# One core, long convolution plus token MLP: shift copies and norm subtractions go to GpSimd, one token group's output pairs go last, and the written order is new

## The chip, the cores and the metric

The kernel runs on one core of a Trainium2 chip. The metric is the device time of one execution in microseconds (us). The engines are TensorE (PE, with its weight loads shown as PEld), VectorE (DVE), ScalarE (ACT), GpSimd (POOL) and SyncE (SP, which issues most DMA transfers). Line numbers are those of the kernel before, as its profile shows them.

## The reference

Two mixers work on the same input x = A_q, of 2048 tokens and 640 features, and a gate blends them:

```python
x = A_q
g = _sigmoid((x * gate_w).sum(-1, keepdims=True))
a = _A_ref(x, A_k, A_v, A_shift_k, A_ssm_k, A_ssm_D)
b = _B_ref(x, B_w1, B_w2, B_w3, B_w4)
return g * a + (1 - g) * b
```

Mixer A filters k along the tokens with four taps, multiplies by v (kv), convolves kv over all tokens with a filter of 2048 taps per feature (in the reference by FFT), adds kv times ssm_D and multiplies by q. Mixer B takes h = gelu(layernorm(x) @ w1), shifts the four quarters of h's features by +1, -1, +2 and -2 tokens, multiplies by w2 and adds x; of this x1 it takes gelu(layernorm(x1) @ w3) @ w4 and adds x1. Weights and inputs are bf16.

## The kernel before

Tokens lie in 16 tiles of 128 partitions, and in four groups sc of four tiles. The steps:

- ln1 normalizes x (statistics on DVE, `bn_math` at line 864 on POOL, with a power -0.5 by `pool_pow` at line 861) and transposes it, by PE for tiles 0 to 7 and by a transposing DMA afterwards.
- mm1 (line 910) is h = gelu(xn @ w1) for five feature tiles of 128. Each of the first four holds 128 features of one quarter; the fifth holds the remaining 32 features of every quarter. The shift of the first four costs nothing, since mm2 reads them at an offset. The fifth has four shifts in one tile, so after its gelu on ACT four copies of 32 partitions go to it at four offsets (line 924, on DVE): 24 copies in all, 16 of 256 columns and 8 of 512.
- mm2(t) (line 945) is x1 = x + h @ w2; it reads the fifth feature tile with its copies. ln2(t) normalizes x1: `ln_math` (line 868) makes -mean, mean squared less epsilon, the difference (line 872, a DVE instruction of one column), and its power -0.5, in 128x1 instructions on POOL but for that one; tiles 0 to 7 are then scaled on DVE, the rest on ACT.
- mm3 and mm4 (lines 976 and 997) are the MLP of 1536 features. `base` (line 992) scales x1 by 1 - g and stores it to the output; mm4's result is scaled on ACT and added to the output by an accumulating POOL transfer (line 1005). Where a half of a tile is not stored by `base` ("summed" is false), mm4 adds x1 by a matmul with the identity.
- The convolution is a transform over blocks of 512 tokens: h_load, h_fold and h_chunk for the filter, kv_block, x_fwd and combine for kv, in two halves hh of 320 features. unit(hh, c) multiplies block c with the filter's blocks on DVE (128x2560 products); two of its sums are accumulating POOL transfers inside SBUF (line 1029).
- final(hh, c, q, k) (line 1053) is the inverse transform of a pair of token tiles, 4c+q and 4c+3-q: two blocks of four matmuls, an ACT copy, two DVE additions, a flip by one matmul with a reversed identity, an ACT copy with the gate's scale, a DVE product with q. For k < 12 the pair is added to the output by an accumulating POOL transfer (line 1078). The last four, k = 12 to 15, are added on DVE to the scaled mm4 result that lies in SBUF, and stored by SP (lines 1080 and 1081); for k = 14 and 15 these last steps are done tile by tile. k goes through hh = 0, then 1, and in each through c = 3, 2, 1, 0.

All operations are recorded first. The order in which each engine runs them is a list, SEQUENCE, written out by hand: `schedule` (line 271) walks it with a model of durations, which gives PSUM banks and some extra waits, and `emit` writes the instructions in that order, each with the semaphore waits that its data need. Every engine works in order, so an instruction that waits holds all behind it. Nearly all instructions have a helper's line: tt 669, ts 674, act 679, mm 689, dma 237 (plain) and 234 (transposing).

Of the kernel before, what the change touches and what calls it, by code (L numbers as in the profile page):

```python
# [8 lines left out]
ACTF = mybir.ActivationFunctionType  # L9
# [3 lines left out]
class Op:  # L13
    __slots__ = ("idx", "eng", "fns", "ins", "outs", "dur", "bias", "nbytes", "preds", "succs", "rank",
                 "tp", "early", "cost", "free", "grp", "tile", "ordinal", "waits", "inc", "value", "dsem", "dval", "snap", "snapd", "start", "end", "order", "lat")

    def __init__(self, idx, eng, fns, ins, outs, dur, bias, nbytes):
        self.idx = idx
        self.eng = eng
        self.fns = fns  # L20
        self.ins = ins
        self.outs = outs
        self.dur = dur
        self.bias = bias
        self.nbytes = nbytes
        self.preds = {}
        self.succs = []
        self.inc = False
        self.dsem = None
        self.tp = False  # L30
        self.early = False
        self.cost = 0.0
        self.lat = 0.0
        self.free = None
        self.tile = None
# [87 lines left out]
def regions(ap):  # L123
# [29 lines left out]
    out = set()  # L153
    for lo, hi in runs:
        b0, b1 = (f0 + lo) * esz, (f0 + hi) * esz
        for q in range(p0 // 32, (p0 + pcnt - 1) // 32 + 1):
            out.add(("SB", q, b0, b1))
# [16 lines left out]
class Prog:  # L174
# [51 lines left out]
    def dma(self, queue, out, in_, bias=0.0, transpose=False, slow=False, free=None, early=False, accum=False, fn=None):  # L226
# [11 lines left out]
        issue = (350.0 + n / 90.0) if transpose else (970.0 if queue == "pool" else 470.0)  # L238
# [5 lines left out]
        op.cost = n * esz / 256 * 1.65 if transpose else n * esz / run * ((46 + 0.087 * run) if accum else (8 + 0.0435 * run)) / 16  # L244
# [26 lines left out]
    def schedule(self, sequence, backlog=3000.0):  # L271
# [4 lines left out]
        done = []  # L276
        avail = [0.0] * 8
# [4 lines left out]
        for i in sequence:  # L282
            o = ops[i]
            st = max([free[o.eng]] + [ops[p].end + d for p, d in delays[i]])
            if o.nbytes and not o.tp and not o.early:
                st = max(st, dfree - backlog)
            t = o.tile
# [15 lines left out]
            if o.nbytes:  # L303
                dfree = max(st + 0.5 * o.dur, dfree) + o.cost
                o.end = max(dfree, o.end) + o.lat
                if o.cost > 500 and not o.tp and not o.early:
# [157 lines left out]
def bass_gated_mix__ssm_conv_h3__mixer_s_mlp__prompt_kernel(  # L464
# [33 lines left out]
    def ps(n, cls):  # L498
# [3 lines left out]
    SEQUENCE = [2, 3, 10, 11, 12, 31, 6, 57, 8, 1, 13, 14, 15, 16, 17, 18, 19, 20, 21, 22, 23, 24, 25, 7, 9, 0, 4, 28, 5, 56, 29, 63, 58, 64,  # L502
# [482 lines left out]
    def summed(hh, t):  # L985
        return 8 * hh + 2 * (3 - t // 4) < KACC
# [200 lines left out]
```

## Time and profile before

| what | value |
|---|---|
| median of the runs shown | 235.55 us (234.9 to 235.9, 3 runs) |
| profiled execution, device time | 235.56 us |
| profiled execution, span | 233.8 us |
| granted TensorE clock, mean | 0.994 |
| ACT busy, instructions | 170.3 us, 317 |
| POOL busy, instructions | 105.9 us, 122 |
| DMA, mean | 195 GB/s |

The span is the time from the first to the last instruction. Busy time counts an engine's own work, not its waiting. A group of instructions has the form: line, engine, operation, out<-in with shapes, xcount, then busy us, mean ns of one, and idle time of the engine just before them with what ended it. In a timeline the columns are start, length, engine, line, operation, with idle time before in square brackets. A row of the waits reads: who waited, for whom, total us, times, longest.

### The profile page before, as it was taken

Reading aid. Unit: us, or ns where it says so; the run is one execution under the profiler, and the core shown is the slowest. Engines: PE = TensorE matmul, PEld = TensorE weight load, DVE = VectorE, ACT = ScalarE, POOL = GpSimd, SP = SyncE. Lnnn points to the kernel's source line nnn. Section 1 sums busy time; section 2 is a strip of 40 time slices with the busy share of each in tenths; the row PEclk is TensorE's granted clock in tenths of the full one; section 3 lists DMA queues with packets and bytes.
Section 4 is the critical chain, followed back from the end, with each engine's and each line's share of the span. In section 5 each row is a group of like instructions: output and inputs, shape, how many; then the busy total and the mean of one; then the engine's idle time right before and its main releaser. Section 6 shows DMA issues by size and latency. Waiting matters only on the chain.

```text
span 233.8 us, 4171 instructions
## 1 busy us (share of the span) xinstructions
PE 221.1 (95%) x1501; PEld 134.6 (58%) x1501; DVE 220.1 (94%) x402; ACT 170.3 (73%) x317; POOL 105.9 (45%) x122
## 2 busy tenths in 40 slices
PE   7999999989998999999999999999999999999960
PEld 2598665436554656544775456654666556776630
DVE  6998999999988999998999999999989999979994
ACT  2799699488796899769949897577655387288881
POOL 0330406274495801196376693246024332456870
PEclk9999999999999999999999999999999999999997
DMA  5999959898878999978638988999978987989998
GB/s 161 360 345 250 253 146 271 246 277 204 140 181 176 240 213 317 343 212 180 157 97 145 187 189 163 146 191 206 259 142 145 196 140 142 185 98 111 95 109 165
DMA packets 63785, 45.48 MB, mean 195 GB/s; under 512 B 28818, under 2 KB 59028, under 8 KB 63764
## 3 DMA queue, kind: packets, MB, share of 16 engines
q1 hardware_dynamic: 54748, 33.33, 55.2%
q0 software_dynamic: 8832, 11.80, 34.9%
q8 instruction: 12, 0.20, 0.3%
q10 hardware_dynamic: 184, 0.08, 0.1%
q14 instruction: 9, 0.07, 0.1%
HBM read 24.22 MB, written 6.55 MB: 132 GB/s over the span
## 4 chain that ended last, share of the span: by engine, by line
PE 45%; DVE 9%; POOL 3%; ACT 2%; issue 1%
PE PSall L689 45%; DVE arena L669 8%; ACT arena L679 2%; POOL arena L674 1%; POOL arena L861 1%; POOL arena L669 1%; DVE arena L959 0%; DVE arena L674 0%
## 5 line engine op out<-in xcount | busy, mean ns | idle before, releaser
L689 PE MATMUL PSall<-arena 128*128 128x320 bf16 (+5 forms) x1444 | 213.7, 307 | 5.3 <-DVE arena L669 2.4
L669 DVE TENSOR_TENSOR arena<-arena 128x640 bf16<-128x640 bf16 (+5 forms) x247 | 182.3, 793 | 3.0 <-ACT arena L679 1.9
L689 PEld LDWEIGHTS PSall<-arena 128*128 128x128 bf16 (+1 forms) x1444 | 130.5, 98 | 86.9 <-DVE arena L669 4.2
L679 ACT ACTIVATE arena<-PSall 128x512 bf16<-128x512 f32 (+6 forms) x189 | 107.7, 634 | 29.4 <-PE PSall L689 25.2
L679 ACT ACTIVATE arena<-arena 128x640 bf16<-128x640 bf16 (+4 forms) x62 | 42.2, 703 | 6.7 <-POOL arena L669 2.7
L861 POOL TENSOR_TENSOR arena<-arena 128x1 f32<-128x1 f32 (+1 forms) x26 | 29.3, 1128 | 31.9 <-DVE arena L674 31.5
L674 POOL TENSOR_SCALAR arena<-arena 128x1 f32<-128x1 f32 (+2 forms) x41 | 24.8, 608 | 34.7 <-DVE arena L959 12.0
L237 POOL DMA_DIRECT2D out_dram<-arena x28 | 30.5, 1197 | 20.5 <-ACT arena L679 15.0
L679 ACT ACTIVATE arena<-PSall,arena 128x640 bf16<-128x640 f32 (+1 forms) x32 | 20.6, 658 | 20.0 <-PE PSall L689 19.9
L237 POOL DMA_DIRECT2D arena<-arena x12 | 14.9, 1242 | 32.1 <-DVE arena L669 28.2
L674 DVE TENSOR_SCALAR arena<-arena 128x640 bf16<-128x640 bf16 (+2 forms) x49 | 14.4, 307 | 3.4 <-POOL arena L674 1.6
L857 DVE BATCH_NORM_STATS2 arena<-arena 128x6 f32<-128x320 bf16 x32 | 14.6, 479 | 2.0 <-DMA arena<-in_A_q_dram 1.7
L669 POOL TENSOR_TENSOR arena<-arena 128x1 f32<-128x1 f32 (+1 forms) x11 | 10.3, 943 | 2.9 <-DVE arena L674 2.5
L715 PE MATMUL PSall<-arena 128*128 128x512 bf16 x15 | 5.4, 536 | 1.6 <-DVE arena L711 1.6
L959 DVE SCALAR_TENSOR_TENSOR arena<-PSall,arena 128x640 bf16<-128x640 f32 x8 | 6.4, 808 | 0.1
L924 DVE TENSOR_SCALAR arena<-arena 32x256 bf16<-32x256 bf16 (+1 forms) x24 | 5.9, 244 | 0.5
L679 ACT ACTIVATE PSall<-PSall 128x640 f32<-128x640 f32 x8 | 5.6, 699 | 0.1
L715 PEld LDWEIGHTS PSall<-arena 128*128 128x128 bf16 x15 | 1.9, 132 | 4.6 <-issue 2.5
L903 PE MATMUL PSall<-arena 128*128 128x128 bf16 x40 | 3.6, 219 | 0.3
L718 ACT ACT_TABLE_LOAD x1 | 1.3, 1283 | 2.7 <-issue 2.7
L903 PEld LDWEIGHTS PSall<-arena 128*128 128x128 bf16 x40 | 2.4, 97 | 1.4 <-DVE arena L858 0.4
L858 DVE BATCH_NORM_AGGREGATE arena<-arena 128x2 f32<-128x12 f32 x16 | 3.0, 197 | 0.0
(24 smaller groups left out, 9.6 us busy)
## 6 DMA issues: line engine op xcount, KB each, us to landing
arena<-arena POOLq DMA_DIRECT2D x12, 640.0 KB, 6.3
arena<-in_A_k_dram SPq DMA_DIRECT2D x14, 400.0 KB, 4.1
arena<-in_A_q_dram SPq DMA_DIRECT2D x14, 320.0 KB, 6.9
out_dram<-arena POOLq DMA_DIRECT2D x20, 160.0 KB, 4.2
arena<-in_A_ssm_k_dram SPq DMA_DIRECT2D x5, 512.0 KB, 4.4
arena<-in_A_v_dram SPq DMA_DIRECT2D x16, 160.0 KB, 3.9
arena<-in_B_w_dram SPq DMA_DIRECT2D x1, 1920.0 KB, 8.8
out_dram<-arena SPq DMA_DIRECT2D x10, 160.0 KB, 3.7
```

What stands on the lines that cost most here:

```text
L237: fn = lambda e: e.dma_start(out, in_, **kw)
L669: P.op(eng, lambda e: e.tensor_tensor(o, real(a), real(b), op), [a, b], [o], dve_ns(o, [a, b], 2) if eng == "dve" else 500)
L674: P.op(eng, lambda e: e.tensor_scalar(o, real(a), s1, s2, op0=op0, **({} if op1 is None else {"op1": op1})), [a] + aps, [o], dve_ns(o, [a] ...
L679: P.op("act", lambda e: e.activation(real(o), real(a), f, bias=bias, scale=scale, **({"accum_out": accum} if accum is not None else {})), ...
L689: fns.append(lambda e, l=l, r=r, i=i: e.matmul(real(o), l, r, start=(i == 0), stop=(i == last)))
L715: P.op("pe", lambda e: e.matmul(real(pw), warm[:, 0:128], warm[:, 128:640], start=True, stop=True), [warm], [pw], 427.0 if i < 14 else 216.0)
L857: P.op("dve", lambda e, o=o, i=i: e.bn_stats(o, i), [i], [o], 400)
L858: P.op("dve", lambda e: e.bn_aggr(bna[:, t, :], bns[k]), [bns[k]], [bna[:, t, :]], 120)
L861: P.op("pool", lambda g: g.tensor_tensor(o, a, e, ALU.pow), [a, e], [o], dur)
L903: P.op("pe", [lambda e, c=c, pb=pb, xn=xn: e.transpose(real(pb)[:, 128 * c:128 * (c + 1)], xn[:, 128 * c:128 * (c + 1)], ident) for c in r ...
L924: P.op("dve", lambda e, o=hT[q, 4, c0:c0 + n], i=hx[q, :]: e.tensor_scalar(o, i, 1.0, None, op0=ALU.mult), [hx[q, :]], [hT[q, 4, c0:c0 + n ...
L959: P.op("dve", lambda e: e.scalar_tensor_tensor(x, real(pr), 1.0, x, op0=ALU.mult, op1=ALU.add, accum_out=st[1, 0][:, t:t + 1]), [pr, x], [ ...
```

## The change

1. `mm1`: for groups 1 to 3 the four shift copies are POOL transfers from SBUF to SBUF (16 in all); group 0 keeps its 8 DVE copies.
2. `ln_math`: the subtraction of one column goes from DVE to POOL.
3. `summed(hh, t)` is true for tiles 0 to 11 and false for 12 to 15, in both halves, where it was true everywhere but for the second half of tiles 0 to 7. So `base` and mm4's accumulating transfer leave tiles 12 to 15 out and take all 640 columns elsewhere; x1 of tiles 12 to 15 is added by the identity matmul.
4. `final` runs with k over c = 2, 1, 0 in both halves, then c = 3 in both halves, so that the four pairs summed on DVE are those of tiles 12 to 15.
5. SEQUENCE is a new list. The durations that `schedule` assumes are changed, and it limits the outstanding transfers in its model; regions of SBUF are rounded to 4 bytes when dependencies are found; a gelu waits for the first one.

```diff
 def regions(ap):
...
-        b0, b1 = (f0 + lo) * esz, (f0 + hi) * esz
+        b0, b1 = (f0 + lo) * esz // 4 * 4, ((f0 + hi) * esz + 3) // 4 * 4
...
+        tab = [tjunk[:, 1:2]] if f == ACTF.Gelu_apprx_tanh else []
...
-        ts(s[3], s[1], s[4], None, ALU.subtract)
+        tt(s[3], s[1], s[4], ALU.subtract, eng="pool")
         pool_pow(s[5], s[3], neghalf[:, t:t + 1])
...
                 for g in range(4):
                     c0, q = 2 + SHIFT[g] + t0, slice(32 * g, 32 * (g + 1))
+                    if sc >= 1:
+                        P.dma("pool", hT[q, 4, c0:c0 + n], hx[q, :])
+                        continue
...
     def summed(hh, t):
-        return 8 * hh + 2 * (3 - t // 4) < KACC
+        return t < 12
 
     def tile_rows(t):
-        n = 640 if summed(1, t) else 320
-        return X[:, t, 0:n], out[0, 128 * t:128 * (t + 1), 0:n]
+        return X[:, t, :], out[0, 128 * t:128 * (t + 1), :]
 
     def base(t):
+        if t >= 12:
+            return
...
-        x, o = tile_rows(t)
-        P.dma("pool", o, x, accum=True)
+        if t < 12:
+            x, o = tile_rows(t)
+            P.dma("pool", o, x, accum=True)
...
-        full, gy, ab = qb[k % 8], gyb[k % 8], (abb[k % 4] if k < 12 else abl[k - 12])
+        full, gy, ab = qb[2 * ((2 - c) % 4) + q], gyb[k % 8], (abb[k % 4] if k < 12 else abl[k - 12])
...
-    for hh in range(2):
-        for c in (3, 2, 1, 0):
-            for q in range(2):
-                at(final, hh, c, q, 8 * hh + 2 * (3 - c) + q)
+    k = 0
+    for group in ((2, 1, 0), (3,)):
+        for hh in range(2):
+            for c in group:
+                for q in range(2):
+                    at(final, hh, c, q, k)
+                    k += 1
...
-    SEQUENCE = [2, 3, 10, 11, 12, 31, 6, 57, 8, 1, 13, 14, 15, 16, 17, 18, 19, 20, 21, 22, 23, 24, 25, 7, 9, 0, 4, 28, 5, 56, 29, 63, 58, 64,
...
+    SEQUENCE = [10, 11, 12, 13, 14, 15, 16, 17, 4, 18, 19, 1, 7, 0, 2, 5, 3, 9, 8, 6, 56, 61, 20, 21, 31, 57, 30, 59, 60, 27, 64, 62, 63, 28,
...
```

In the new order PE runs the fifteen warm-up matmuls partly among the first real ones; the inverse matmuls of the first half's groups 2, 1 and 0 stand before the last quarter of mm3; and mm4 of tiles 12 to 15 stands at the end, the last 13 matmuls of tile 12 being PE's last.

More of the change, by code (lines that the diff above doesn't have):

```diff
@@ L14 @@
     __slots__ = ("idx", "eng", "fns", "ins", "outs", "dur", "bias", "nbytes", "preds", "succs", "rank",
-                 "tp", "early", "cost", "free", "grp", "tile", "ordinal", "waits", "inc", "value", "dsem", "dval", "snap", "snapd", "start", "end", "order", "lat")
+                 "tp", "early", "cost", "free", "grp", "tile", "ordinal", "waits", "inc", "value", "dsem", "dval", "snap", "snapd", "start", "end", "order", "lat", "ring")
     def __init__(self, idx, eng, fns, ins, outs, dur, bias, nbytes):
@@ L33, in __init__ @@
         self.lat = 0.0
+        self.ring = 0
         self.free = None
@@ L237, in dma @@
             fn = lambda e: e.dma_start(out, in_, **kw)
-        issue = (350.0 + n / 90.0) if transpose else (970.0 if queue == "pool" else 470.0)
+        issue = (1240.0 + n / 1200.0) if transpose else 970.0 if queue == "pool" else 530.0
         op = Op(len(self.ops), queue, [fn], [in_], [out], issue, bias, n * esz)
@@ L243, in dma @@
         run = esz * min(run_of(out), run_of(in_))
-        op.cost = n * esz / 256 * 1.65 if transpose else n * esz / run * ((46 + 0.087 * run) if accum else (8 + 0.0435 * run)) / 16
+        op.cost = n * esz / 256 * 1.72 if transpose else n * esz / run * ((46 + 0.087 * run) if accum else (8.4 + 0.0457 * run)) / 16
+        op.ring = 0 if queue == "pool" else n * esz // 256 if transpose else n * esz // run
+        if queue != "pool" and op.ring > 200 and not transpose:
+            op.dur = 660.0
         op.lat = 1150.0 if transpose else 3000.0 if accum else 2300.0
@@ L276, in schedule @@
         done = []
+        ring = []
         avail = [0.0] * 8
@@ L286, in schedule @@
                 st = max(st, dfree - backlog)
+            while o.ring and sum(r for e, r in ring if e > st) + o.ring > 2048:
+                st = min(e for e, r in ring if e > st)
             t = o.tile
@@ L305, in schedule @@
                 o.end = max(dfree, o.end) + o.lat
+                if o.ring:
+                    ring.append((dfree, o.ring))
                 if o.cost > 500 and not o.tp and not o.early:
@@ L678, in act @@
         aps = [s for s in (scale, bias) if not isinstance(s, (int, float))]
+        tab = [tjunk[:, 1:2]] if f == ACTF.Gelu_apprx_tanh else []
         P.op("act", lambda e: e.activation(real(o), real(a), f, bias=bias, scale=scale, **({"accum_out": accum} if accum is not None else {})),
-             [a] + aps, [o] + ([accum] if accum is not None else []),
+             [a] + aps + tab, [o] + ([accum] if accum is not None else []),
              n_of(o) / 1.2 + 55 + 93 * len(aps) + (105 if accum is not None else 0) +
@@ L923, in mm1 @@
                     c0, q = 2 + SHIFT[g] + t0, slice(32 * g, 32 * (g + 1))
+                    if sc >= 1:
+                        P.dma("pool", hT[q, 4, c0:c0 + n], hx[q, :])
+                        continue
                     P.op("dve", lambda e, o=hT[q, 4, c0:c0 + n], i=hx[q, :]: e.tensor_scalar(o, i, 1.0, None, op0=ALU.mult),
-                         [hx[q, :]], [hT[q, 4, c0:c0 + n]], n / 3.84 + 65)
+                         [hx[q, :]], [hT[q, 4, c0:c0 + n]], n / 3.84 + 168)
     def mmg(sc):
@@ L959, in mm2 @@
         P.op("dve", lambda e: e.scalar_tensor_tensor(x, real(pr), 1.0, x, op0=ALU.mult, op1=ALU.add, accum_out=st[1, 0][:, t:t + 1]),
-             [pr, x], [x, st[1, 0][:, t:t + 1]], 920)
+             [pr, x], [x, st[1, 0][:, t:t + 1]], 743)
         act(xn2[t % 2], X[:, t, :], ACTF.Square, scale=D ** -0.5, accum=st[1, 1][:, t:t + 1])
```

121 rows, old and new, of the table SEQUENCE are left out of this document.

## Prediction

> **What bounds the kernel now.** I read the page's part 1 first, then the table of windows cut at the stages, then the chain of waits and the waits, then the timeline of the end. Part 1 and the windows (per stretch: length, then busy us and instructions of PE, PEld, DVE, ACT, POOL; granted clock, DMA share, GB/s):
>
> ```profile
> PE 221.1 (95%) x1501; PEld 134.6 (58%) x1501; DVE 220.1 (94%) x402; ACT 170.3 (73%) x317; POOL 105.9 (45%) x122
> ...
> 0.00:20.00 20.00, 18.10 (x205) 12.54 (x206) 16.44 (x63) 13.80 (x36) 4.63 (x12) 1.00 0.96 293
> 20.00:60.00 40.00, 38.38 (x270) 23.83 (x268) 38.90 (x98) 31.43 (x65) 15.95 (x26) 1.00 0.96 225
> 60.00:106.00 46.00, 45.06 (x269) 24.44 (x267) 43.85 (x86) 36.89 (x62) 23.98 (x29) 1.00 0.93 229
> 106.00:208.00 102.00, 101.73 (x639) 62.22 (x638) 99.12 (x106) 70.34 (x123) 46.44 (x44) 1.00 0.85 166
> 208.00:228.00 20.00, 17.52 (x125) 11.56 (x124) 19.09 (x46) 16.88 (x33) 14.60 (x13) 1.00 0.99 107
> ```
>
> Two engines are full. PE is idle 1.62 us in 20 to 60, 0.94 in 60 to 106, 0.27 in 106 to 208 and 2.48 in 208 to 228. From 106 to 208 nothing can be won unless PE gets less work. DVE is nearly as full, so PE's idle time hangs on how far DVE runs ahead. From the waits (total us, times, longest) and the groups:
>
> ```profile
> DVE arena L674 <- POOL arena L674: 1.6, 2, 1.1
> ...
> DVE arena L674 <- ACT arena L679: 1.2, 2, 1.0
> ```
> ```profile
> L674 DVE TENSOR_SCALAR arena<-arena 128x1 f32<-128x1 f32 x20 | 3.9, 194 | 2.8 <-POOL arena L674 1.6 <-ACT arena L679 1.2
> ...
> L924 DVE TENSOR_SCALAR arena<-arena 32x256 bf16<-32x256 bf16 x16 | 3.6, 222 | 0.3
> ...
> L924 DVE TENSOR_SCALAR arena<-arena 32x512 bf16<-32x512 bf16 x8 | 2.3, 287 | 0.2
> ```
>
> Sixteen of the twenty 128x1 instructions are the norm subtractions (line 872). DVE stood 2.8 us at the head of its queue for them, with products behind. The end, PE's rows alone:
>
> ```profile
> 204.79 9.60 PE L689 MATMUL PSall<-arena 128*128 128x320 bf16 x69
> 214.68 9.42 PE L689 MATMUL PSall<-arena 128*128 128x320 bf16 x66 [0.29 <-DVE arena L669]
> 224.34 1.71 PE L689 MATMUL PSall<-arena 128*128 128x320 bf16 x11 [0.23 <-DVE arena L669]
> 227.90 0.45 PE L689 MATMUL PSall<-arena 128*128 128x320 bf16 x2 [1.85 <-DVE arena L669]
> ```
>
> The last pairs are a loop PE, ACT copy, two DVE additions, flip matmul, and nothing else is left for PE to do meanwhile: it stands 2.37 us. Then 5.4 us pass from 228.35 to the end at 233.77. A 320-column matmul is shown 299 ns long, but back to back they take 64.1/452 = 0.142 us (groups of 106.6 to 208), so a stall is about 0.16 us longer than shown.
>
> **The change, part by part.** All sums go against the profiled execution: 235.56 us, its span 233.77, so 1.8 around it; the median of the runs shown is 235.55.
>
> Work. The matmuls are the same 1501: tiles 12 to 15 get the residual matmul in both halves (8) where tiles 0 to 7 had it in one (8); twelve pairs still end in an accumulating store and four are summed on DVE. Bytes accumulated by mm4 stay: 8 x 80 + 8 x 160 KB before, 12 x 160 now, four transfers fewer, and four base scalings (823 ns on ACT) and stores (SP) go. ACT was waiting for PE 45.1 us in all, so that is worth nothing.
>
> DVE loses 8 copies of 222 ns (1.8 us), 8 of 287 (2.3) and 16 subtractions of 194 (3.1): 7.2 us by the rows, about 5 once the overlap with the next instruction is taken off (the 68 products of 1485 ns sum to 101.0 and are busy 98.4; short ones overlap more). The 2.8 us of idle time before the subtractions go too, since POOL now waits for POOL. So DVE is 7 to 8 us lighter, of 220. It does not shorten the time by itself: it lengthens DVE's lead over PE. PE's idle 1.62 + 0.94 + 0.27 = 2.83 us of 20 to 208 (lines 669, 674 and ACT fed by them are the releasers) is what can go. If the cover were whole, all of it; if the new order spoils it, nothing. I take **2.2**, near the upper end, because DVE's relief is three times the stalls.
>
> POOL gains 16 transfers at 1.2 us (nearest row, its DMA issues, mean 1197 ns), 16 subtractions at 1.06 (its 128x1 tensor_tensor, mean 1062), and loses four issues: 105.9 + 19 + 17 - 5 = 137 us, 60% of the span. A subtraction is not on PE's path where the norm is early: in the new order POOL's four norm steps of tiles 0 to 7 stand far ahead of the use of their results in mm3. If that cover is gone, it costs 1.06 - 0.19 per tile.
>
> Does POOL's added work slow DVE? Groups of DVE in 120 to 140, where POOL was busy 14.9 of 20 us, then in 160 to 170, where it was busy 1.6 of 10:
>
> ```profile
> L669 DVE TENSOR_TENSOR arena<-arena 128x2560 bf16<-128x2560 bf16 x12 | 17.3, 1487 | 0.0
> ```
> ```profile
> L669 DVE TENSOR_TENSOR arena<-arena 128x2560 bf16<-128x2560 bf16 x4 | 5.9, 1488 | 0.0
> ```
>
> 1487 against 1488 ns: DVE pays nothing; POOL pays (line 861 runs 0.56 to 4.2 us). The Trainium skill, GPSIMD Engine Reference, Specifications, speaks against the change here: the two share SBUF interfaces, with contention when DVE has two SBUF inputs, as these products have. The trace shows that contention falls on POOL; by the page taken as a DVE cost the gain would be smaller, by the row it is not.
>
> Shift copies. Each becomes gelu (ACT 0.6 us), issue, landing, ahead of mm2. Three of the four groups have over 10 us of matmuls before the first mm2 that reads them. The tight one is token group 2: after its fifth feature tile PE has 20 matmuls of 512 columns and 21 of 320, 20 x 0.23 + 21 x 0.142 = 7.6 us, until mm2(7), which needs two copies, and 12 x 0.142 = 1.7 more until mm2(9), which needs all four. POOL does 4 x 1.2 with two norm steps of 0.6 between: 0.6 + 4.8 + 1.2 = 6.6 us before landing. No row shows a plain small POOL transfer. Landing lies between 1.9 us (the plain 80 KB store of SP) and 8.9 (the longest accumulating POOL transfer). So mm2(9) is early by 0.8 or late by 6.2; I take 3.5, between the plain one and POOL's medians of 4.2 and 4.3, nearer the latter: **0.8 late**. By the Trainium skill, DMA: Bandwidth & Descriptors, section Anatomy of one DMA, a GpSimd transfer takes 2.0 us and little more for 32 KB; by that the loss would be none and the sum 230.3.
>
> The end. Now mm4 of tiles 13, 14 and 12 stands among the last pairs; two blocks of 13 matmuls (1.8 us each) come around the last two flips. Of the stall of 2.37 us shown (2.85 with three modelled ends) a remainder of some 0.45 us may stay, one flip matmul's loop less its block (ACT 0.70, DVE 2 x 0.32 and two hand-overs, against 1.8): I take **2.4**. After the last matmul there is now one ACT copy (row 128x640 with scale, 790 ns), a DVE addition of 128x640 (482) and one of 128x320 (320), two SP issues (0.45 each, five take 2.50 with their waits) and the landing, 2.2 (233.77 less the last issue's end, 231.53): 4.7 against 5.4, **0.7**.
>
> Sum: 235.6 - 2.2 - 2.4 - 0.7 + 0.8 = **231.1 us**.
>
> **Rivals.**
> - *All stalls go* and no copy is late: 235.6 - 2.83 - 2.85 - 0.7 = 229.2; with the modelled ends of some ten stalls (1.6) 227.6. For it: DVE's relief. Against: every instruction stands in a new order, and the old one lost 2.83 us in places that looked no worse.
> - *A new wait in the middle.* The pairs of groups 2, 1, 0 (first half) move ahead: the first inverse matmul stands behind 1067 matmuls instead of 1236, so the units they need must be ready about 170 matmuls, some 30 us, sooner. DVE then leads by a few us where it led by tens. It idled 6.8 us up to 106 (windows: 3.56 + 1.10 + 2.15), and 2.8 of that goes; the other 4.0 against a lead of a few us makes it late by 1 to 3: 232 to 234. Against: its 5 us of spared work lie before that place too.
> - *The change does not do what it says*: summing on chip saves nothing (counts above), the tail merely swaps one last loop for another and the middle stays: within 0.5% of 235.6.
> - *Slower: accumulating transfers late.* The twelve of line 1029 sit in POOL's in-order queue, now among four-step norms instead of three. Each lands 2.7 to 8.9 us after its issue (median 6.3) and DVE has 6 to 10 us of work until it reads the sum. Every us of POOL delay beyond cover stops DVE, then PE: 12 x 1 = 12 us gives 243; it decides from 12 x 0.5 = 6, which takes 231.1 past 236.7. For it: POOL at 60%. Against: POOL waited 28.2 us for DVE there, up to 8.4 at a time:
>
> ```profile
> POOL arena L237 <- DVE arena L669: 28.2, 8, 8.4
> ```
>
> **How the numbers follow.** Forecast 231.1: 0.50 (229.5 to 232). All stalls go: 0.17. New wait in the middle: 0.12. No gain: 0.08. Slower: 0.13 (236.7 and more, some of it near 237). A measurement can tell 0.5% (1.2 us) from no change. Faster by over 0.5%: 0.50 + 0.17 + 0.12 = 0.79; same 0.08; slower 0.13. The range runs from all stalls gone, 227.6, to 236.2, where the late copies at their upper end (231.1 - 0.8 + 6.2 = 236.5) nearly lie; the slower case and a little of the best are left out.
>
> **What would show it.** Right: PE idle in the last 20 us under 1 us, no DVE idle time before norm instructions, 4.7 us from last matmul to end, products still 1487 ns. Shift: a PE or PEld wait on a POOL-issued transfer near 50 to 56 us. Middle: PE waiting for line 669 around 150 to 180. Slower: DVE waiting for the accumulating transfers. Wrong if PE's idle time before 106 us grows, since that part of the order is wholly new, and counts of instructions bound its waits but do not time them.

## The result and the profile after

The changed kernel is slower. Its median is 242.02 us (241.48 to 244.64, 4 runs) against 235.73 (234.90 to 236.17, 4 runs) for the kernel before beside it: a ratio of 1.029 with a 95% interval of 1.021 to 1.038. The forecast was 231.1 us with a range of 227.6 to 236.2, so sign and range are both wrong. The profiled execution took 241.58 us, its span is 239.7. (The profiles of three experiments below, shift copies back on DVE and the two with the norm chain on DVE, are of executions over 1.5% above the fastest of their kernel; of those the places of the waits count, and their sizes only roughly.)

Lines have moved: tt is 677, ts 682, act 688, mm 698, plain dma 238, transposing dma 235, pool_pow 870, the shift copy 936. First the page's part 1, then rows of part 2 (the span in 40 slices of 6 us, busy tenths and clock), both of the kernel after:

```profile
PE 221.7 (93%) x1501; PEld 135.6 (57%) x1501; DVE 214.3 (89%) x370; ACT 170.5 (71%) x313; POOL 114.0 (48%) x150
...
PE   7999999999999999999979299959999999999991
...
PEclk9999999999999999999999979999999999999998
```

DVE is 5.8 us lighter, as the change meant. But PE, which was nearly full from 60 us on, has holes in the 21st, 23rd and 27th slice, that is in 120 to 126, 132 to 138 and 156 to 162 us. The table of windows of the kernel after (length, then busy us of PE, PEld, DVE, ACT, POOL; clock, DMA share, GB/s):

```profile
0.00:20.00 20.00, 17.84 (x204) 12.50 (x205) 16.75 (x67) 13.72 (x35) 4.71 (x12) 1.00 0.95 297
20.00:60.00 40.00, 39.32 (x297) 24.99 (x295) 38.50 (x82) 35.13 (x71) 27.40 (x44) 1.00 1.04 227
60.00:106.00 46.00, 46.00 (x259) 25.14 (x258) 44.12 (x81) 39.67 (x64) 19.55 (x33) 1.00 0.99 237
106.00:160.00 54.00, 44.66 (x271) 26.22 (x268) 45.71 (x44) 31.15 (x57) 29.46 (x33) 0.97 0.92 159
160.00:208.00 48.00, 47.55 (x287) 28.06 (x288) 44.16 (x48) 33.10 (x60) 19.03 (x19) 1.00 0.88 159
208.00:234.00 26.00, 26.00 (x192) 18.62 (x191) 23.84 (x50) 16.92 (x32) 13.50 (x12) 1.00 0.89 119
```

PE's idle time, length less busy, is 0.68 us in 20 to 60 (before 1.62), nothing in 60 to 106 (0.94), nothing from 208 until the last matmul (2.48 to 228). All of that was forecast. In 106 to 208, where before 0.27 us were lost, it is 9.34 + 0.45 us. So the question is one stretch, 120 to 160. The waits, then PE's and ACT's timelines there, all of the kernel after:

```profile
ACT arena L688 <- DMA arena<-arena: 18.4, 3, 10.1
...
PEld PSall L698 <- ACT arena L688: 13.8, 9, 5.8
...
PE PSall L698 <- ACT arena L688: 10.3, 4, 5.3
...
ACT arena L688 <- POOL arena L677: 3.4, 4, 2.2
```
```profile
125.40 7.62 PE L698 MATMUL PSall<-arena 128*128 128x320 bf16 x35 [1.44 <-ACT arena L688]
138.31 19.19 PE L698 MATMUL PSall<-arena 128*128 128x512 bf16 x107 [5.28 <-ACT arena L688]
160.45 4.73 PE L698 MATMUL PSall<-arena 128*128 128x320 bf16 x30 [2.95 <-ACT arena L688]
```
```profile
122.88 1.78 ACT L688 ACTIVATE arena<-arena 128x640 bf16<-128x640 bf16 x2 [2.24 <-POOL arena L677]
...
127.89 1.18 ACT L688 ACTIVATE arena<-PSall 128x512 bf16<-128x512 f32 x2
136.13 0.74 ACT L688 ACTIVATE arena<-arena 128x640 bf16<-128x640 bf16 x1 [7.07 <-DMA arena<-arena]
```

PE waits for ACT, and ACT stands for 7.07 us at one instruction: the square in mm2 of tile 14, which writes its junk output into the buffer xn2[0]. There were two such buffers for all tiles, and xn2[0] still held tile 12's normalized rows, which a transposing DMA was reading. Behind the square in ACT's queue lay the evictions of PSUM that PE needed for mm3. The same happens once more, 10.13 us at tile 15. The smaller wait of PE, 1.44 us at 124, is another matter: there ACT stood 2.24 us for POOL's norm operations. The chain of waits of the kernel after says the same in the other direction. Before 126 us it goes through those operations of POOL (119.42 to 125.73); from there to the end nothing else of length lies on it:

```profile
125.76 0.95 ACT arena L688 x2
126.70 9.35 DMA arena<-arena
136.13 2.13 ACT arena L688 x4
138.31 6.19 PE PSall L698 x20
...
148.06 10.74 DMA arena<-arena
...
160.45 73.92 PE PSall L698 x478
```

Why did a transpose take 9.35 us, where one in the kernel before took 2.6? The issues of transfers in 120 to 140 us (count, KB, median us from issue to landing), kernel after first, kernel before second:

```profile
arena<-arena POOLq DMA_DIRECT2D x2, 640.0 KB, 9.3
out_dram<-arena POOLq DMA_DIRECT2D x3, 160.0 KB, 3.7
arena<-arena SPq DMA_TRANSPOSE x3, 9.3
```
```profile
arena<-arena POOLq DMA_DIRECT2D x2, 640.0 KB, 6.3
...
arena<-arena SPq DMA_TRANSPOSE x2, 2.6
```

In both kernels two sums of a unit are accumulated by POOL transfers there. The medians hide something: of the transposes only one in each row has a landing in the trace (tile 12's after, 9.35 us), and the two accumulating transfers of the kernel after took 11.5 us, issued at 126.29 beside that transpose, and 7.1 us, issued at 139.70 without one.

The packets in the trace (a transfer moves in many small pieces) show the difference. Before, the 640 packets of a transpose, 256 bytes each, started within 0.9 us (122.45 to 123.36, and again 128.96 to 129.87), and the 256 packets of an accumulating transfer, 2560 bytes each, within 3.5 and 3.8 us (from 124.54 and from 131.03); they took turns. After, one of each was under way together. The transpose's packets spread over 7.2 us (128.18 to 135.34) and the other's over 8.7 us (128.54 to 137.22), and from 129 to 135 us one accumulating packet took 350 to 870 ns on average, counted microsecond by microsecond, instead of some 225 to 255. Together the two needed about twice what they need one after the other.

The end of the kernel after (ACT, DVE and SP):

```profile
234.29 2.34 SPq L238 DMA_DIRECT2D out_dram<-arena  x4
234.39 0.79 ACT L688 ACTIVATE arena<-PSall,arena 128x640 bf16<-128x640 f32 x1 [0.96 <-PE PSall L698]
235.22 0.73 DVE L677 TENSOR_TENSOR arena<-arena 128x640 bf16<-128x640 bf16 x2 [0.72 <-ACT arena L688]
```

PE ends at 234.35 and the span at 239.70: 5.35 us, where 5.4 passed before.

### The profile page after: what moved, and what is told of

The parts are those of the page before. It is cut to its first block, busy times and chain, and to the rows that moved or that the text cites. A ratio compares the mean times of both kernels' runs of the same rounds, so it can differ in the third digit from the quotient of the medians.

```text
span 239.7 us, 4146 instructions
## 1 busy us (share of the span) xinstructions
PE 221.7 (93%) x1501; PEld 135.6 (57%) x1501; DVE 214.3 (89%) x370; ACT 170.5 (71%) x313; POOL 114.0 (48%) x150
## 4 chain that ended last, share of the span: by engine, by line
PE 77%; DMA 10%; ACT 4%; POOL 3%; DVE 2%; issue 1%; SPq 1%; DVEq 0%; ACTq 0%; POOLq 0%
PE PSall L698 76%; DMA arena<-arena 8%; ACT arena L688 4%; POOL arena L677 2%; DMA arena<-in_A_q_dram 2%; POOL arena L870 1%; DVE arena L677 1%; PE PSall L912 1%; SPq L238 1%; POOL arena L238 1%; DVE arena L866 1%; DVE arena L682 0%; DVEq L1174 0%; PE PSall L724 0%; ACTq L419 0%
## 5 line engine op out<-in xcount | busy, mean ns | idle before, releaser
L698 PE MATMUL PSall<-arena 128*128 128x320 bf16 (+4 forms) x1444 | 214.7, 309 | 10.5 <-ACT arena L688 10.3
L698 PEld LDWEIGHTS PSall<-arena 128*128 128x128 bf16 x1444 | 131.7, 98 | 93.0 <-ACT arena L688 13.8
L688 ACT ACTIVATE arena<-PSall 128x512 bf16<-128x512 f32 (+6 forms) x189 | 109.0, 631 | 23.6 <-PE PSall L698 20.3
L688 ACT ACTIVATE arena<-arena 128x640 bf16<-128x640 bf16 (+3 forms) x58 | 41.4, 735 | 22.8 <-DMA arena<-arena 18.4
L238 POOL DMA_DIRECT2D arena<-arena x28 | 25.6, 917 | 45.0 <-DVE arena L677 35.6
L682 POOL TENSOR_SCALAR arena<-arena 128x1 f32<-128x1 f32 (+2 forms) x41 | 26.7, 654 | 29.3 <-DVE arena L971 10.9
L238 POOL DMA_DIRECT2D out_dram<-arena x24 | 27.6, 1215 | 10.9 <-DVE arena L677 7.7
L870 POOL TENSOR_TENSOR arena<-arena 128x1 f32<-128x1 f32 (+1 forms) x26 | 25.5, 983 | 8.7 <-DVE arena L682 7.6
L677 POOL TENSOR_TENSOR arena<-arena 128x1 f32<-128x1 f32 (+1 forms) x27 | 16.5, 616 | 26.2 <-ACT arena L688 25.5
L682 DVE TENSOR_SCALAR arena<-arena 128x640 bf16<-128x640 bf16 (+2 forms) x33 | 11.5, 361 | 0.0
L724 PEld LDWEIGHTS PSall<-arena 128*128 128x128 bf16 x15 | 1.7, 128 | 4.0 <-issue 2.4
L912 PEld LDWEIGHTS PSall<-arena 128*128 128x128 bf16 x40 | 2.5, 98 | 1.0 <-DVE arena L682 1.0
L936 DVE TENSOR_SCALAR arena<-arena 32x256 bf16<-32x256 bf16 x8 | 1.8, 221 | 0.3 <-ACT arena L688 0.2
```

The source lines that it names most:

```text
L238: fn = lambda e: e.dma_start(out, in_, **kw)
L677: P.op(eng, lambda e: e.tensor_tensor(o, real(a), real(b), op), [a, b], [o], dve_ns(o, [a, b], 2) if eng == "dve" else 500)
L682: P.op(eng, lambda e: e.tensor_scalar(o, real(a), s1, s2, op0=op0, **({} if op1 is None else {"op1": op1})), [a] + aps, [o], dve_ns(o, [a] ...
L688: P.op("act", lambda e: e.activation(real(o), real(a), f, bias=bias, scale=scale, **({"accum_out": accum} if accum is not None else {})), ...
L698: fns.append(lambda e, l=l, r=r, i=i: e.matmul(real(o), l, r, start=(i == 0), stop=(i == last)))
L724: P.op("pe", lambda e: e.matmul(real(pw), warm[:, 0:128], warm[:, 128:640], start=True, stop=True), [warm], [pw], 427.0 if i < 14 else 216.0)
```

## The experiments

Theory A, after the result: transposes (SP) and POOL's transfers that are under way together slow each other several times, and it becomes PE's wait because xn2 has two buffers. Theory B: POOL's longer norm chain, in a queue with the issues of transfers, makes ACT late. Theory C: it is the order of ACT and SP alone. All medians and ratios are against the kernel before on the same chip.

### Own buffers for tiles 13 to 15

```diff
-    xn2 = [V(oXN + 640 * i, 640) for i in range(2)]
+    xn2 = {t: V(oXN + 640 * (t % 2), 640) if t < 13
+           else V(oKV + 2048 + 640 * (t - 12), 640) for t in range(NT)}
```
The space is kv's, dead by then; mm2 and ln2 of 13 to 15 are recorded after kv's last use, and SP issues the transposes of 14 and 15 right behind their ACT operation. Every transfer stays.

> The changed kernel with one edit: tiles 13, 14 and 15 have normalized-row buffers of their own in dead space, instead of the two that alternate, so that ACT need not wait for a transposing transfer before it squares or normalizes the next tile (the transposes of tiles 14 and 15 are issued directly behind their ACT instruction). All transfers stay. Theory A, transposes and POOL-issued transfers that run together crawl, and ACT waits for the landing because there are only two buffers: PE's stalls of about 5.3 us near 132 and 3.1 us near 157 go, the landings stay at 9 to 20 us, and the time falls from 242 to 232 to 234 us. Theory B, the norm chain on POOL behind the accumulating transfers is what ACT waits for: the waits move from DMA to POOL and the time stays within 2 us of 242. Theory C, ACT's or SP's new order alone: the same as B.

Measured: 235.35 us (233.87 to 239.06), ratio 0.998 (0.994 to 1.001), 6.7 us less than the kernel after. Tile 12's transpose still crawls (12.3 us), but nobody waits for it. What remains, in PE's timeline of this run:

```profile
126.39 8.93 PE L698 MATMUL PSall<-arena 128*128 128x320 bf16 x40 [1.44 <-ACT arena L688]
136.11 2.46 PE L698 MATMUL PSall<-arena 128*128 128x512 bf16 x10 [0.80 <-ACT arena L688]
138.98 2.33 PE L698 MATMUL PSall<-arena 128*128 128x512 bf16 x10 [0.41 <-ACT arena L688]
```

The waits of 5.28 and 2.95 us are gone, as Theory A has it; the time is 1.4 us above its range, because of the waits that remain. Theories B and C had 242 staying. PE's, DVE's and ACT's orders are those of the kernel after but for a few neighbours. So the price of the crawl hung on there being only two buffers.

### The unit sums of the first half on DVE

```diff
+                if hh == 0:
+                    tt(o, o, t, ALU.add)
+                    continue
                 P.dma("pool", ..., accum=True)
```

> The changed kernel, but the six accumulating transfers inside SBUF of the first half's units are additions on DVE (6 x 1.48 = 8.9 us more for DVE, no such transfer between 115 and 170 us). Theory A: the transposes of tiles 9 to 13 land 2.6 to 5 us after issue instead of 9 to 23, ACT's wait for transfers of 18.4 us falls under 3, PE has no stall over 1 us at 125 to 160; the time is 232 to 240, as DVE's 8.9 us are partly on the path. Theory that the transposes are slow because the transfer engines are simply full: landings shorten by less than half. Theory B (norm chain on POOL): landings may shorten, PE's stalls stay.

Measured: 239.93 us (239.51 to 240.68), ratio 1.019 (1.015 to 1.023). The issues in 120 to 140 us of this run:

```profile
arena<-arena SPq DMA_TRANSPOSE x3, 3.2
```

The run's waits have this row, where the kernel after has 18.4:

```profile
ACT arena L688 <- DMA arena<-arena: 1.9, 3, 0.9
```

9.35 became 3.2 us (again one landing on record) with no other transfer changed, and ACT's waits for arena transfers fell from 18.4 to 1.9 us. This is the direct evidence that the unit transfers made the transposes crawl. The time moved less, because six sums more on DVE made the units late: PE waits 5.79 us at 159 for ACT, which waits 6.5 for DVE. Theory A had expected no such stall.

### Parts undone in the kernel after

Shift copies back on DVE (`if sc >= 4` for `if sc >= 1`):

> The changed kernel with the 16 shift copies back on DVE (same order). Theory A: the stalls at 125 to 160 stay, so the time stays at 240 to 243; the 0.84 us PE wait before mm2 of tile 7 near 53 us goes, the transposes of 44 to 51 us land in 2.6 to 4.5 us instead of 5 to 7, and DVE is 4 us busier. Rival, the shift copies are what costs the 6 us (by POOL's queue or by contention handed on): 235 to 237.

Measured: 243.05 us (242.41 to 246.89), ratio 1.031 (1.026 to 1.035). The two large waits stay (3.69 at 136, 3.32 at 160), so the shift copies are not their cause. The wait at 53 us before mm2 of tile 7 goes, and others come, for DVE (1.14 at 55) and for ACT (1.13 at 67).

The subtraction back on DVE (`ts(s[3], s[1], s[4], None, ALU.subtract)`):

> The changed kernel with the norm subtraction of one column back on DVE (same order). Theory A: within 1.5 us of the changed kernel (242), the waits for the transposes stay. Theory B, POOL's four-step norm chain is the cause: 236 to 238, POOL's and ACT's waits around 118 to 148 shrink.

Measured: 244.27 us (242.37 to 246.42), ratio 1.034 (1.027 to 1.040). The wait of 1.44 us at 124 is gone, as Theory B has it for that wait alone; the two others are 6.61 and 4.21 us, larger than in the kernel after. So the longer norm chain on POOL is not the main cause. But the second of them is no longer mainly the transposes' doing: before it ACT stands 5.84 us for POOL, whose norm waits for DVE, and then 2.59 us for a transpose that lands after 3.2.

Both undone, so that only the last group at the end and the new order are left:

> The kernel after with both moves to POOL undone (16 shift copies and the norm subtraction on DVE again): what is left is the last token group's pairs at the end, summed on chip, and the new order. Theory A (the middle's loss comes from the order, which lets transposes and the accumulating transfers of the units run together, and from xn2's two buffers): the two large PE waits near 130 and 155 us stay, 242 to 246 us, and the tail of the last 70 us is as in the kernel after. Rival (the loss comes from POOL's added work): the waits go, 233 to 236.

Measured: 248.00 us (246.38 to 249.18), ratio 1.049 (1.042 to 1.055), above even the range that Theory A gave. Its waits and two stretches of its windows:

```profile
ACT arena L688 <- DMA arena<-arena: 12.5, 3, 7.2
...
PE PSall L698 <- ACT arena L688: 9.6, 4, 5.5
```
```profile
142.00:146.00 4.00, 3.66 (x9) 1.34 (x10) 3.93 (x4) 4.00 (x8) 2.21 (x3) 0.50 0.82 119
...
163.00:167.00 4.00, 3.92 (x15) 2.25 (x16) 4.00 (x4) 1.43 (x3) 1.22 (x1) 0.50 0.42 76
```

PE waits 5.45 us at 137 and 3.71 at 159, and in the 4 us behind each its granted clock is half. The first wait is the crawl again (ACT stands 7.24 us for a transpose that lands after 9.5). Before the second ACT stands 4.77 us for POOL and 3.16 for a transpose that lands after 3.8, so that one is not the crawl, other than Theory A has it. The loss is therefore in the order, with the last group's move, which needs it, and the smaller changes of point 5 of the list of changes. In that order the two moves to POOL together help by 6 us (248.00 against 242.02); each undone alone cost 1.0 and 2.3 us, less than these intervals can tell. It was not split further, since in the old order these four pairs come first.

### Parts alone in the old order

The 16 shift copies as POOL transfers, the kernel before otherwise:

> The kernel before, in its own order, with one part of the change alone: the 16 shift copies of token groups 1 to 3 (32x256 each) go as transfers that POOL issues instead of DVE operations. Theory A (transposes that SP issues and transfers that POOL issues slow each other while they run together): the ln1 transposes of tiles 8 to 15 land in 5 to 7.5 us where they took 2.6 to 4.4, the copies land in over 5 us where they meet them, and the matmuls of mm2 of tiles 7 to 9 are late by about 1 us; some of the 1 us stalls of 38 to 72 us may go, since DVE is freed; 235 to 237.5 us. Rival (small transfers are harmless beside transposes): transposes stay at 2.6 to 4.4 us, DVE's 16 x about 168 ns come off, 233.5 to 235.

Measured: 244.31 us (243.19 to 245.38), ratio 1.037 (1.032 to 1.042): far outside both expectations. PE's waits are 1.53 at 29, 1.60 at 52 and 4.17 at 78. The chain of waits of this run before the last of them:

```profile
75.59 0.54 POOL arena L237
76.12 0.02 issue
76.15 1.95 POOL arena L861
78.10 0.47 POOL arena L669
78.56 3.36 DMA arena<-arena
81.93 0.09 issue
82.02 2.35 PE PSall L689 x7
```

The transposes hardly suffer (median 3.6 us in 24 to 70, before 2.6). The copy is late because it stands behind a power of 1.95 us in POOL's queue and then takes 3.4 us to land, in an order that gave a DVE copy 0.22. Theory A does not explain this run; a longer path does. PE's three waits are 7.3 of the 8.9 us lost, and behind the longest its granted clock is half (0.50 in 82 to 86 us).

The subtraction alone on POOL:

> The kernel before, in its own order, with one part alone: the subtraction in the norm chain is done on POOL instead of DVE. Theory B (POOL's longer chain makes ACT late for late tiles): stalls of 0.5 to 2 us appear on PE between 100 and 160 us, 236 to 238 us. Theory A alone: no change but a few tenths, 235 to 236.

Measured: 233.88 us (232.90 to 236.27), ratio 0.993 (0.989 to 0.998): 0.7% faster, a small gain that is clear of the noise, against both expectations. Two windows of this run:

```profile
20.00:60.00 40.00, 39.77 (x279) 24.82 (x278) 39.47 (x94) 32.54 (x67) 19.47 (x33) 1.00 1.01 230
60.00:106.00 46.00, 45.33 (x266) 24.57 (x268) 43.98 (x80) 39.05 (x68) 26.44 (x33) 1.00 0.98 239
```

PE's idle time in 20 to 106 us is 0.23 + 0.67 instead of 1.62 + 0.94. This is the greater part of the forecast's first term by itself: the waits of DVE for POOL's 128x1 results ahead of its products (1.6 us in the kernel before) are gone from the waits.

### The waits that are left

With own buffers, and the second norm's whole chain of tiles 8 to 15 but the power on DVE:

```diff
+        eng = "dve" if l == 1 and t >= 8 else "pool"
```

> The run with own xn2 buffers for tiles 13 to 15 (which came to 235.35 us), and in addition all three small operations of the second norm's chain of tiles 8 to 15 on DVE; only the power stays on POOL. Theory B for what was left there (PE waits of 1.60, 0.97, 0.58 and 0.38 us between 124 and 141 us come from POOL's chain): these go, 232 to 233 us. Rival (they come from the order of ACT and SP, Theory C): they stay, 235 to 236, DVE's new waits for ACT add to it.

Measured: 241.85 us (237.77 to 243.21); no ratio, since its runs lie too far apart. Inconclusive for Theory B: the changed durations in `schedule`'s model gave it other extra waits (a large transfer waits for the one that the model has landed last), among them one of POOL's addition of mm4 for tile 3 on tile 12's transpose. In the profiled execution that transpose landed after 11.5 us, POOL stood 7.11 us for it, the norm chain behind POOL, ACT behind that, and PE waited 6.34 us at 138. Theory A again, with another engine holding the wait.

> As the run with own buffers and the chain on DVE, and the shift copies of token group 1 back on DVE (groups 2 and 3 stay transfers). Theory A at 53 us (mm2 of tile 7 waits 1.45 us for shift copies that run together with ln1's transposes): the wait goes, DVE's eight copies cost it up to 1 us near 40 to 50 us; 1 us under the run without it, 231 to 232. Rival (DVE is the bound there): the wait moves to DVE's evictions and the time stays within 0.5 us.

Measured: 241.08 us (237.36 to 242.66), ratio 1.015 (1.005 to 1.025), with the same 6.34 us. The wait at 53 us stayed (1.04): it belongs to the copies of group 2, not of group 1, so this was the wrong group.

Then own buffers, also for tile 11, POOL as in the kernel after, PSUM banks as in the run with own buffers, and ACT's and SP's order changed:

```diff
-    xn2 = {t: V(oXN + 640 * (t % 2), 640) if t < 13
-           else V(oKV + 2048 + 640 * (t - 12), 640) for t in range(NT)}
+    xn2 = {t: V(oXN + 640 * (t % 2), 640) if t < 11 or t == 12
+           else V(oKV + 2048 + 640 * max(t - 12, 0), 640) for t in range(NT)}
 order of ACT and SP: the ln2 application and transpose of tile
-9, 12, 11, 14 where their POOL chain was planned to end
+9 behind mm4-1, 12 behind mm2-11, 11 and 14 behind mm3-1's evictions
```

> The run with own xn2 buffers (235.35 us), tile 11 given an own buffer too, and only ACT's and SP's order changed: the second norm's application of tiles 9, 12, 11 and 14 is placed behind the evictions of PSUM that PE waits for (behind mm4-1, mm2-11 and the mm3-1 evictions), and its transpose behind it. All transfers and POOL's chain stay. Theory C for what was left (ACT stands at the head of its queue for POOL's chain while finished PSUM banks wait behind it): PE's waits of 1.60, 0.97, 0.58 and 0.38 us between 124 and 141 us go, 232 to 233 us. Theory A for what was left (the waits move with the transfers): new waits of about the same size appear where the later transposes meet POOL's transfers, 234.5 to 236.

Measured: 232.50 us (231.81 to 233.77), ratio 0.988 (0.982 to 0.993). It is the best kernel of all, 9.5 us below the kernel after. PE's timeline of this run around the old holes (mm is line 704 there, act 694):

```profile
124.92 7.86 PE L704 MATMUL PSall<-arena 128*128 128x512 bf16 x36 [0.44 <-ACT arena L694]
133.16 5.34 PE L704 MATMUL PSall<-arena 128*128 128x512 bf16 x24 [0.38 <-ACT arena L694]
139.50 18.62 PE L704 MATMUL PSall<-arena 128*128 128x320 bf16 x123 [1.00 <-ACT arena L694]
159.21 11.13 PE L704 MATMUL PSall<-arena 128*128 128x512 bf16 x62 [1.08 <-ACT arena L694]
```

The place is as Theory C has it: 1.44 + 0.80 + 0.41 us became 0.44 + 0.38. But 1.00 and 1.08 appear further on, and PE's waits for ACT add up to 3.3 us in both runs. Where the time went shows when the starts of the same weight loads are compared, one profiled run with the other. The run with ACT's order changed is ahead by 0.9 us after the first 10 us, gains 1.0 at 53 us, where the order of ACT was not touched, gains 2.3 between 117 and 158 us, and loses 1.0 of it until the last matmul. So some 1.3 us of the 2.9 between the medians come from the stretch that was changed; the rest lies elsewhere and may not be due to the order. Nor is it Theory C alone: tile 12's transpose landed after 6.5 us instead of 12.3. So the kernel after lacks buffers above all, and it gains by an ACT order that puts evictions ahead of waits for POOL.

> As the run with ACT's order changed, and the four shift copies of token group 2, whose landing 6 us after their issue made mm2 of tile 7 wait 1.45 us at 53 us, back on DVE. Theory A at 53 us: without these copies the ln1 transposes of 44 to 51 us land in 2.6 to 4.4 us instead of 5 to 7.7, the wait goes, 0.8 to 1.5 us under the run without it. Rival: DVE (0.17 to 0.2 us for each copy, all four in a stretch where DVE has no gap) takes over, within 0.4 us.

Measured: 235.85 us (234.69 to 237.68), ratio 1.002 (0.998 to 1.006). The ln1 transposes of 43 to 56 us land in 3.9 us (median) instead of 5.2, as Theory A has it, though the kernel before had 4.4 with no POOL transfer there at all (few of them have a landing: two, three and one). The wait that was to go was hardly there: in the profiled execution of the run that this one starts from, PE waits 0.26 us at 53 (1.29 with own buffers alone). And DVE is late instead: PE waits 1.02 at 55, 1.13 at 66 and 0.59 at 71. In this order the four copies belong on POOL.

## Why the prediction was wrong, step by step

- **DVE's relief: right.** Forecast about 5 us net, measured 220.1 - 214.3 = 5.8. The products kept their length (1484 ns in 120 to 140 us), so POOL's added work costs DVE nothing. That the contention falls on POOL instead, as the prediction reads the spread of its power, no run separates from other causes.
- **PE's stalls up to 106 us: right, the 0.8 in it by luck.** 2.56 us of idle time became 0.68, and that 0.68 (0.84 with the modelled end of a matmul) is the wait at 53 us, forecast as 0.8 for late shift copies. It came before mm2 of tile 7, not tile 9; the second copy landed at 54.16 and PE went on at 54.25, though the profile puts the end of the wait down to an ACT operation that ended 0.04 us later still. Four other runs with these copies on POOL have 0.26, 0.52, 1.29 and 1.84 us there. Two sizes in it were off and cancelled: an issue took about 0.67 us, (25.6 - 14.9)/16 from the groups, not 1.2; the landing of the 32 KB copies had a median of 5.9 us in 24 to 70 (4.1 for those of 16 KB), not 3.5. The Trainium skill, DMA: Bandwidth & Descriptors, section Anatomy of one DMA, would have given an estimate of some 2.1 us and no wait; the trace disagrees, 5.9 us for 32 KB beside transposes, and 3.8 in the run with the shift copies alone.
- **The tail: right.** 2.48 us of idle time went entirely (forecast 2.4).
- **The end: mis-sized.** 5.35 us instead of 4.7. ACT's 0.79 and DVE's 0.73 are as forecast; the last landing took 239.70 - 236.63 = 3.07 us, not 2.2.
- **"If the cover were whole, all of it; if the new order spoils it, nothing", taken as 2.2 us: the step that failed.** I priced a spoiled order at no gain, so its worst price was put at nothing without a reason. From 106 to 208 us, where 0.27 us were lost, it cost 9.79 us of waits, and PE's busy time grew by 0.6 us, with matmuls at half clock behind the first wait. What took the time is the cost of transposes and accumulating transfers that are under way together, passed on to PE by two buffers. The account closes: 235.6 - 1.88 - 2.48 - 0.08 + 9.52 + 0.6 + 0.26 (the start) = 241.5, measured 241.58.
- **The rivals.** None had this mechanism. The slower one named the right stream, the accumulating transfers of the units, and by chance the right size, 243, but the wrong victim: DVE waiting for their sums. DVE waited for such a transfer once, 1.8 us; the transposes beside them were late, and ACT, which I had written off with 45.1 us of waiting, held the chain. The new wait in the middle was looked for at 150 to 180 us behind DVE; it came at 123 to 160 behind ACT. The sign of being wrong that the prediction names, more idle time of PE before 106 us, did not show either: the loss came behind it.
- **What I did not look at:** which transfers of the new order meet, and how many buffers let a late one be harmless. The orders of SP and POOL were known; that the landing of a transpose depends on what POOL has under way was visible in the kernel before only as its absence.
- **POOL's load** was forecast as 137 us and is 114.0: besides the issues, a subtraction took about 0.44 us, (15.6 - 8.5)/16, not 1.06. It did not matter.

What stays open: why the two streams slow each other as much as they do. One experiment (the sums on DVE) shows that the unit transfers cause it; nothing here shows what happens inside the DMA engines, and no experiment varied which of the two starts first (see the last section). Nor was the new order taken apart further than that.

## What to carry to other kernels

When an order changes, list which transfers will be under way at the same time and which buffer each holds, not only which instruction follows which: the loss came from a reader two steps behind a transfer that nobody had counted as slow. An instruction that waits for a buffer or for another engine's chain should not stand in ACT's queue ahead of evictions that PE needs; own buffers brought 6.7 us here, and the swap 2.9 more, of which the profiles show some 1.3 in the place that it changed. And a part that is good by itself, or bad, need not be so in another order: the shift copies on POOL cost 8.9 us in the old one, and in the new one they save between nothing that can be measured (242.02 against 243.05) and some 4 us (244.27 against 248.00, with the subtraction on DVE).

## What the runs showed of the hardware

- A transpose issued by SP and a large accumulating transfer issued by POOL, under way together, took 9.35 and 11.5 us to land in the kernel after, against 2.6 to 3.2 and 6.0 to 6.5 apart; with own buffers it was 12.3 and 11.6. The Trainium skill, DMA: Bandwidth & Descriptors, section Issuing engines are not separate DMA queues, says that transfers of all engines run on the same 16 DMA engines and interleave. The trace agrees in that packets of both kinds start in the same microseconds, and adds that the two together can take about twice as long as one after the other.
- It is not always so. In that kernel, and in the four other runs with such a pair near 130 us that both took over 9 us to land, the transpose's first packet comes 0.15 to 0.5 us ahead of the accumulating transfer's. In the run with ACT's order changed the accumulating transfer's comes first, by 0.7 us: its packets kept 229 to 274 ns in the three us that both were under way, it landed after 7.2 us and the transpose after 6.5. The traces show this; no run was made to test it.
- Beside the small shift copies transposes lost less: 5.2 us (median) in 43 to 56 of the run with ACT's order changed, 3.9 with the four copies there back on DVE.
- A wait of PE has a second price. Behind the wait of 5.28 us the kernel after shows this window, while behind the one of 2.95 us the clock stayed at 1.00:

```profile
138.00:142.00 4.00, 3.69 (x10) 1.27 (x11) 3.12 (x3) 4.00 (x8) 4.00 (x5) 0.57 0.87 132
```

The run with order and group alone has 0.50 behind waits of 5.45 and 3.71 us (windows above), and the run with the shift copies back on DVE has it behind its wait of 3.32:

```profile
163.57:167.57 4.00, 4.00 (x16) 2.27 (x17) 3.93 (x4) 2.03 (x3) 3.84 (x4) 0.50 1.05 274
```

So the limit lies between 2.95 and 3.32 us of wait here. By the clock records in the traces the half rate lasted 3.4 us in the kernel after and 6.8 us in the other three cases. The Trainium skill, TensorE: Matmul & The Clock Gate, Part 1, has half rate after an idle window of about 3.4 us; the runs are near it, since a wait of 3.32 us is 3.48 with the modelled end of a matmul.
